# The second block's attention probabilities: transposed by VectorE and a trip through DRAM in place of TensorE

## The chip, the cores and the metric

The kernel runs on one core of a Trainium2 chip. The metric is the time of the program on the device, in microseconds (us); the median over a few runs is compared. TensorE multiplies matrices and writes to PSUM; VectorE, ScalarE and GpSimd (POOL in the rows) work element by element; SyncE (SP) issues the DMA transfers here, in the order of its queue.

## The reference

Three stages follow each other. Attention over 4 sequences of 576 positions, 8 heads of 64, where a position sees itself and the 63 before it:

```python
scores = scale * np.matmul(q, k.transpose(0, 1, 3, 2))
mask = (rel >= 0) & (rel < 64)
scores = np.where(mask, scores, -1e9)
attn = softmax(scores)                  # over the last axis
attn_out = np.matmul(attn, v)
```

Its output, 2304 tokens of 512 numbers, goes through `softplus(x @ w_in) @ w_out` with 2048 inner numbers, and then through `(sigmoid(x @ w_gate) * (x @ w_val)) @ w_out2` with 1536. The weights come in as 64-bit floats, all else as 32-bit floats.

## The kernel before

**The work and its tiles.** The 2304 tokens of the first two stages are cut into blocks of 512, 384, 384, 512 and 512 tokens (L21). For each block and each of 16 slices of the inner dimension there are two slots of TensorE work: a projection (`m1_proj`, L415) and, two slices later, the output product (`m1_out`, L438), each 12 matmuls. Matmuls are done as three products of values split in a high and a low part (`mm3`, L393). The list `slots` (L589 to L614) holds this order; slots 0 to 29 are block 0's but for its last two products, and slot 30 is block 1's first projection. The third stage follows, with a scheme of seven products in place of eight.

**The weights.** Two slices of weights at a time are loaded by SP (`w_load`), and turned from 64-bit floats to 32-bit floats by ScalarE (`w_scale`) and VectorE (`w_shift`, `w_sign`, `w_low`, L159 to L174); then ScalarE casts the high part (`w_hi`, L179) and VectorE subtracts it to give the low part (`w_lo`, L187). For the first stage's 32 slices all of this happens while block 0 runs.

**The attention** goes by groups of 64 queries, all heads at once; block 1 has six groups, 8 to 13, in three pairs. While one block's slots run, the next block's attention is done between them. A group is a chain: scores on TensorE (`att_scores`, L281), scale, mask and maximum on VectorE (`att_max`, L303 and L306), exponentials on ScalarE (`att_exp`, L316), sums and reciprocals on VectorE (`att_sum`, L324 and L325), normalization on GpSimd (`att_norm`, L330). Then the probabilities have to be transposed, in one of two ways:

- *near*, for blocks 0 and 1: four transposes on TensorE into PSUM (`att_transpose`, L338) and a copy from PSUM to SBUF by ScalarE or VectorE (`att_copy`, L367);
- *far*, for block 2 and on (`FAR = 2`, L26): VectorE transposes blocks of 32x32 (`att_blocks`, L346), SP sends the result to DRAM (`att_send`, L352), and SP fetches it in another order by up to four transfers (`att_fetch`, L359), so that the whole is transposed.

After this come the product with the values (`att_values`, L376) and the split of its output into the next block's input (`att_hi`, L384, and `att_lo`, L389). Block 0's own attention is done ahead of the slots, in another set of PSUM banks. Group 9 begins a sequence and has 64 keys in place of 128, so it has half the work in most steps. Scores, near transposes and value products of block 1 and on share two PSUM banks (`at`). The far way's 32x32 result has one buffer (`pd`), normalized probabilities have two.

**The order.** Everything but the slots is first put at a slot by hand. `attention(g, t, far)` (L649) hangs a group's steps on slot `t` and those after it: for the near way the transposes at t + 6 and the values at t + 8, for the far way the block transpose at t + 5 (t + 7 for the pair's second group), the send one slot later, the fetch three after that, and the values at t + 13. The loop at L670 chooses `t` for each pair of a block. Then, for all that lies ahead of the third stage, `lead_in` (L944) plans the order on each engine anew. It takes each step's price, engine, dependencies and buffers from `traits` (L786), goes through the engines' time step by step, and takes among the steps that can start soonest the one with the smallest rank. The rank of a step of weights is worked back from the slot that needs them; the rank of a step of block 1's attention is the time of the slot at which it was put. The engines then run in the order so found, each waiting at its head. What `traits` says of a group's scores and of the buffer of its probabilities depends on `turned(g)` (L781): the step that empties the probabilities, the TensorE transpose or the block transpose.

Of the kernel before, what the change touches and what calls it, by code (L numbers as in the profile page):

```python
# [22 lines left out]
LAG = 2  # L23
LEAD = 7
COMBO0, COMBO = 36, 9.8
FAR = 2  # L26
RG = 1.1
HURRY = 1.0
SLACK, NEAR = 0.15, .3
# [12 lines left out]
def tile_kernel(ctx: ExitStack, tc: tile.TileContext, qk, vt, w1, w2, wg, wv, wo, out):  # L42
# [576 lines left out]
    def at(slot, order, fn, *args):  # L619
        events[slot].append((order, len(events[slot]), fn, args))  # L620
# [28 lines left out]
    def attention(g, t, far):  # L649
        at(t, 20, att_scores, g)  # L650
        at(t + 1, -30, att_max, g)
        at(t + 2, -30, att_exp, g)
        near, odd = g < NG0, g % 2
        at(t + 4 - near, -33, att_sum, g)
        at(t + 4 - near, -32, att_norm, g)
        if far:
            at(t + 5 + 2 * odd, -31, att_blocks, g)
            at(t + 6 + 2 * odd, -61, att_send, g)
            at(t + 9 + 2 * odd, -61, att_fetch, g)
            e = t + 13  # L660
        else:
            e = t + 6 if near else t + 8
            at(e - 2, 21, att_transpose, g)
            at(e - 1, -31, att_copy, g)
        at(e - 4, -59, v_load, g)
        at(e, 22, att_values, g)
        at(e + 1, -29, att_hi, g)
        at(e + 1, -28, att_lo, g)

    for b in range(1, NB1):  # L670
        s0, s1 = pos[m1_proj, b - 1, 0], pos[m1_proj, b, 0]
        ng, g0 = BLOCKS1[b] // Q, starts1[b] // Q
        for j in range(ng):
            far = b >= FAR
            first = -3 if far else 9
            t = s0 + first + (s1 - s0 - (14 if far else 15 + first)) * (j // 2) // max(ng // 2 - 1, 1)
            attention(g0 + j, t, far)
            at(t - 4, -60, qk_load, g0 + j)

# [17 lines left out]
    def used_last(slot):  # L697
        return max(pos[m1_proj if kind == "w1" else m1_out, NB1 - 1, f]
                   for (kind, f), _ in seq1[slot - slot % 2:slot - slot % 2 + 2])

    for f in range(NF2):
        t, i = COMBO0 + int(COMBO * f), len(seq1) + 2 * f
# [12 lines left out]
    for f in range(NF2):  # L715
        i = WO_AT + f
        t = end + (-7, -1)[f] if f < 2 else pos[m2_out, 0, f - 2, 0] - 1
# [11 lines left out]
    for s in range(NS2):  # L729
        t = last + 2 if s == 0 else pos[m2_prod, s - 1, 3, 0]  # L730
# [5 lines left out]
    for k in range(7):  # L736
        for kc in range(2):
            t = max(used_last(2 * k + kc) + 1, last + 18 + k)
# [26 lines left out]
    first = -int(RG * NG0) - 6  # L765
    for g in range(NG0):
        t = int(first + RG * g)
# [13 lines left out]
    def turned(g):  # L781
        return (att_blocks if grp_block[g][0] >= FAR else att_transpose, g)

# [293 lines left out]
```

## Time and profile before

| | |
|---|---|
| runs | 894.48, 894.54, 895.28 us; median 894.54 |
| profiled execution | span from the first to the last instruction 892.8 us; the page gives no other time for it |
| TensorE clock | granted at full speed (2.4 GHz) throughout |
| instructions | 13509 |
| TensorE matmuls | 884.1 us busy, 99% of the span |
| VectorE | 523.7 us, 59% |
| ScalarE | 399.6 us, 45% |
| GpSimd | 153.7 us, 17% |
| the chain that ended last | TensorE 98%, ScalarE 1%, VectorE 1% |
| DMA | 177.59 MB, mean 199 GB/s |

The page is one profiled execution. Busy shares are means over the span, whose stretches differ, and TensorE's busy time is modelled from pipelined matmuls: the start of one to the start of the next is what one costs. What a change in one stretch is worth is read from the rows of that stretch, and from which wait ends last there. In a row of the timeline the start and the duration stand ahead of the engine; a bracket gives the idle time of the engine before it, and who ended it.

### The profile page before, as it was taken

The numbers are of one execution on the slowest core, as the hardware profiler recorded it, in microseconds if no ns is written. First come the engines' busy times: TensorE is split into PE (matmuls) and PEld (weight loads), VectorE is DVE, ScalarE is ACT, GpSimd is POOL, SyncE is SP. The second block draws the span as 40 slices with busy tenths as digits, with TensorE's granted clock in tenths as the row PEclk, the third lists the DMA queues.
The fourth block names the chain that finished last, engine by engine and source line by source line (L and its number), as shares of the span: only waits on it lengthen the run. The fifth ranks groups of instructions, "written<-read, shape, count | busy, mean of one in ns | idle before, by whom it ended". The sixth has DMA issues, their size and how long they took to land.

```text
span 892.8 us, 13509 instructions
## 1 busy us (share of the span) xinstructions
PE 884.1 (99%) x5033; PEld 796.5 (89%) x5035; DVE 523.7 (59%) x921; ACT 399.6 (45%) x892; POOL 153.7 (17%) x157
## 2 busy tenths in 40 slices
PE   9999999999999999999999999999999999999998
PEld 7688789999999888888889999999999999999997
DVE  5898876556555656365515667668445447444444
ACT  6867857546764755345323333334222225222222
POOL 4001102102110220002001333331111112111110
PEclk9999999999999999999999999999999999999999
DMA  9946346766786775683306565545454445544441
GB/s 348 395 158 207 134 163 211 248 198 229 265 270 208 239 235 163 212 284 130 130 1 255 221 256 201 206 176 216 178 212 156 161 163 208 185 165 165 165 166 72
DMA packets 56211, 177.59 MB, mean 199 GB/s; under 512 B 6096, under 2 KB 21456, under 8 KB 51536
## 3 DMA queue, kind: packets, MB, share of 16 engines
q1 hardware_dynamic: 56000, 176.58, 55.9%
q8 instruction: 40, 0.66, 0.3%
q14 instruction: 27, 0.22, 0.1%
q10 hardware_dynamic: 144, 0.13, 0.0%
HBM read 139.72 MB, written 36.96 MB: 198 GB/s over the span
## 4 chain that ended last, share of the span: by engine, by line
PE 98%; ACT 1%; DVE 1%; POOL 0%; issue 0%; POOLq 0%
PE h L394 17%; PE h L396 17%; PE h L395 17%; PE acc L394 11%; PE acc L395 11%; PE acc L396 11%; PE at L289 3%; PE at L376 2%; PE at L396 2%; PE at L395 2%; PE at L394 2%; PE acc L289 1%; PE h L406 1%; PE acc L338 0%; ACT w L179 0%; POOL w L330 0%
## 5 line engine op out<-in xcount | busy, mean ns | idle before, releaser
L512 DVE TENSOR_TENSOR w<-h,w 128x384 f32<-128x384 f32 x216 | 117.1, 556 | 159.5 <-PE h L396 156.8
L394 PE MATMUL h<-w,wc 128*128 128x384 f32 x504 | 169.0, 335 | 0.1
L396 PE MATMUL h<-w,wc 128*128 128x384 f32 x504 | 168.9, 335 | 0.0
L395 PE MATMUL h<-w,wc 128*128 128x384 f32 x504 | 168.7, 335 | 0.0
L524 POOL TENSOR_TENSOR g<-w,g 128x384 fp32r<-128x384 f32 x70 | 73.9, 1056 | 296.7 <-ACT g L517 252.1
L394 PE MATMUL h<-xt,w 128*128 128x512 f32 (+1 forms) x320 | 119.4, 373 | 0.6 <-ACT w L179 0.5
L394 PE MATMUL acc<-g,w 128*128 128x512 f32 (+1 forms) x320 | 119.5, 374 | 0.0
L396 PE MATMUL h<-xt,w 128*128 128x512 f32 (+1 forms) x320 | 117.9, 368 | 1.0 <-DVE w L187 1.0
L396 PE MATMUL acc<-g,w 128*128 128x512 f32 (+1 forms) x320 | 117.7, 368 | 0.0
L395 PE MATMUL acc<-g,w 128*128 128x512 f32 (+1 forms) x320 | 117.6, 368 | 0.0
L395 PE MATMUL h<-xt,w 128*128 128x512 f32 (+1 forms) x320 | 117.6, 368 | 0.0
L436 DVE TENSOR_TENSOR g<-h,g 128x512 fp32r<-128x512 f32 (+1 forms) x80 | 50.7, 634 | 82.9 <-ACT g L430 82.6
L394 PEld LDWEIGHTS h<-w,wc 128*128 128x128 f32 x504 | 94.6, 188 | 2.3 <-DVE w L512 0.4
L395 PEld LDWEIGHTS h<-w,wc 128*128 128x128 f32 x504 | 94.6, 188 | 2.0
L396 PEld LDWEIGHTS h<-w,wc 128*128 128x128 f32 x504 | 94.6, 188 | 0.0
L423 ACT ACTIVATE h<-h 128x512 f32<-128x512 f32 (+1 forms) x80 | 43.2, 540 | 106.6 <-PE h L396 104.4
L517 ACT CAST g<-w 128x384 fp32r<-128x384 f32 x72 | 36.9, 513 | 118.5 <-DVE w L512 118.5
L396 PEld LDWEIGHTS h<-xt,w 128*128 128x128 f32 x320 | 60.0, 188 | 9.5 <-DVE w L187 2.0
L394 PEld LDWEIGHTS h<-xt,w 128*128 128x128 f32 x320 | 60.1, 188 | 9.0 <-ACT w L179 0.6
L394 PEld LDWEIGHTS acc<-g,w 128*128 128x128 f32 x320 | 60.1, 188 | 8.0
L396 PEld LDWEIGHTS acc<-g,w 128*128 128x128 f32 x320 | 60.1, 188 | 7.7
L330 POOL TENSOR_TENSOR p<-p,st 128x512 f32<-128x512 f32 (+1 forms) x28 | 27.8, 996 | 226.8 <-DVE st L325 151.4
(129 smaller groups left out, 1438.5 us busy)
## 6 DMA issues: line engine op xcount, KB each, us to landing
wc<-wcd SPq DMA_DIRECT2D x36, 1792.0 KB, 7.2
qk<-in_qk SPq DMA_DIRECT2D x28, 512.0 KB, 4.8
wcd<-raw SPq DMA_DIRECT2D x24, 512.0 KB, 3.3
w<-in_w SPq DMA_DIRECT2D x16, 512.0 KB, 9.4
raw<-in_w SPq DMA_DIRECT2D x16, 512.0 KB, 4.6
v<-in_vt SPq DMA_DIRECT2D x25, 256.0 KB, 3.7
raw<-in_wg SPq DMA_DIRECT2D x12, 512.0 KB, 4.7
raw<-in_wv SPq DMA_DIRECT2D x12, 512.0 KB, 6.1
```

Of the source, the lines that this page charges most:

```text
L289: nc.tensor.matmul(out=s[:, j, :w], lhsT=t[:, 0, j, :], rhs=t[:, 1, j, :w], start=g >= NG0, stop=g >= NG0 or j == NPAIR - 1)
L330: nc.gpsimd.tensor_tensor(out=p[:, :, :w], in0=p[:, :, :w], in1=st[:, 2, :].unsqueeze(2).to_broadcast([P, NPAIR, w]), op=ALU.mult)
L376: nc.tensor.matmul(out=o[h * Q:(h + 1) * Q, j, :], lhsT=v[:w, (2 * j + h) * Q:(2 * j + h + 1) * Q], rhs=pt[:w, h, j], start=True, stop=True)
L394: nc.tensor.matmul(out=o, lhsT=lh, rhs=rh, start=first, stop=False)
L395: nc.tensor.matmul(out=o, lhsT=lh, rhs=rl, start=False, stop=False)
L396: nc.tensor.matmul(out=o, lhsT=ll, rhs=rh, start=False, stop=last)
L406: nc.tensor.matmul(out=idle["out"], lhsT=t[:, 0, :P], rhs=t[:, 1], start=True, stop=True)
L423: nc.scalar.activation(out=t, in_=t, func=AF.Softplus)
L436: nc.vector.tensor_tensor(out=g[:, 1, :n], in0=t, in1=g[:, 0, :n].bitcast(F32), op=ALU.subtract)
L512: nc.vector.tensor_tensor(out=out, in0=a, in1=b, op=op)
L517: nc.scalar.copy(out=g[:, 0, :HALF], in_=t)
L524: eng.tensor_tensor(out=g[:, 1, :HALF], in0=t, in1=g[:, 0, :HALF].bitcast(F32), op=ALU.subtract)
```

## The change

`FAR` becomes 1, so that block 1's six groups take the far way too, and `turned` and the planner's prices with it. The loop that chooses the slots gets numbers of its own for block 1: the three pairs start at slots 3, 6 and 10, where they started at 9, 12 and 15; their values are put at slots 16, 19 and 23, where they were at 17, 20 and 23. Blocks 2 to 4 keep their slots. The loads of queries and keys are put four slots ahead of the scores, as before.

```diff
--- before.py
+++ after.py
@@ -23,7 +23,7 @@
 LAG = 2
 LEAD = 7
 COMBO0, COMBO = 36, 9.8
-FAR = 2
+FAR = 1
 RG = 1.1
 HURRY = 1.0
 SLACK, NEAR = 0.15, .3
@@ -672,8 +672,8 @@
         ng, g0 = BLOCKS1[b] // Q, starts1[b] // Q
         for j in range(ng):
             far = b >= FAR
-            first = -3 if far else 9
-            t = s0 + first + (s1 - s0 - (14 if far else 15 + first)) * (j // 2) // max(ng // 2 - 1, 1)
+            first = -3 if b > 1 else 3
+            t = s0 + first + (s1 - s0 - (14 if b > 1 else 20 + first)) * (j // 2) // max(ng // 2 - 1, 1)
             attention(g0 + j, t, far)
             at(t - 4, -60, qk_load, g0 + j)
 
```

## Rows read from the trace of the kernel before

**Rows 1.** The page: busy time, share of the span and instructions.

```profile
PE 884.1 (99%) x5033; PEld 796.5 (89%) x5035; DVE 523.7 (59%) x921; ACT 399.6 (45%) x892; POOL 153.7 (17%) x157
```

**Rows 2.** Stretches: length, busy time (instructions) by engine, PEclk, DMA share, GB/s.

```profile
46.60:88.60 42.00, 42.00 (x219) 34.73 (x219) 39.90 (x61) 29.70 (x63) 1.97 (x3) 1.00 0.52 182
...
94.00:129.00 35.00, 34.77 (x222) 28.57 (x223) 28.75 (x44) 23.08 (x44) 2.04 (x2) 1.00 0.52 181
```

**Rows 3.** Timeline of TensorE, and one row of VectorE: start, duration, instruction.

```profile
35.64 1.89 PE L289 MATMUL at<-qk 128*128 128x128 f32 x16
...
96.66 1.95 PE L289 MATMUL at<-qk 128*128 128x128 f32 x16
98.36 0.48 PE L394 MATMUL acc<-g,w 128*128 128x512 f32 x1
...
116.78 0.42 DVE L389 TENSOR_TENSOR xt<-at,xt 128x256 fp32r<-128x256 f32 x1
...
129.07 0.33 PE L394 MATMUL h<-xt,w 128*128 128x384 f32 x1
```

**Rows 4.** Waits from 30 to 130 us (last row: whole span): total, times, longest.

```profile
ACT w L160 <- DMA w<-in_w: 1.7, 2, 0.9
...
PE h L396 <- DVE w L187: 1.0, 1, 1.0
...
PE h L394 <- ACT w L179: 0.5, 1, 0.5
...
SPq L135 <- DVE w L173: 41.1, 8, 12.6
...
DVE pd L346 <- DMA pd<-pd: 4.9, 2, 4.3
```

**Rows 5.** Timeline of TensorE around the wait and an earlier projection.

```profile
85.35 0.50 PE L394 MATMUL h<-xt,w 128*128 128x512 f32 x1
...
94.23 0.50 PE L396 MATMUL h<-xt,w 128*128 128x512 f32 x1 [0.96 <-DVE w L187]
```

**Rows 6.** Timeline of VectorE, 69 to 96 us.

```profile
69.94 0.69 DVE L436 TENSOR_TENSOR g<-h,g 128x512 fp32r<-128x512 f32 x1 [1.37 <-ACT g L430]
...
81.52 0.68 DVE L303 SCALAR_TENSOR_TENSOR p<-at,mask 128x512 f32<-128x512 f32 x1
82.24 0.69 DVE L306 TENSOR_REDUCE st<-p 128x4 f32<-128x512 f32 x1
...
84.76 0.68 DVE L187 TENSOR_TENSOR w<-w,w 128x512 fp32r<-128x512 f32 x1
...
89.43 0.43 DVE L389 TENSOR_TENSOR xt<-at,xt 128x256 fp32r<-128x256 f32 x1 [0.78 <-ACT xt L384]
...
93.50 2.60 DVE L187 TENSOR_TENSOR w<-w,w 128x512 fp32r<-128x512 f32 x4
```

**Rows 7.** Block 1's transposes (median ns in the middle), and one group's neighbours in time.

```profile
L338 PE MATMUL at<-ident,p x24: 270/272/273, 76.5 to 111.8; 128*128 128x128 f32 x20, 128*64 128x128 f32 x4
...
108.07 0.39 PE L396 MATMUL acc<-g,w 128*128 128x512 f32 x1
108.30 0.60 PE L338 MATMUL at<-ident,p 128*128 128x128 f32 x4
108.66 0.48 PE L394 MATMUL h<-xt,w 128*128 128x512 f32 x1
108.97 0.40 PE L395 MATMUL h<-xt,w 128*128 128x512 f32 x1
```

**Rows 8.** The copies of the transposed probabilities.

```profile
L367 ACT COPY pt<-at x6: 580/590/604, 77.1 to 112.1; 128x512 f32<-128x512 f32 x5, 64x512 f32<-64x512 f32 x1
```

**Rows 9.** The later blocks' block transposes, sends and fetches: ns minimum/median/maximum.

```profile
L359 SPq DMA_DIRECT2D pt<-pd x84: 303/427/1682, 136.3 to 365.7; - x84
L346 DVE STREAM_TRANSPOSE pd<-p x22: 445/699/711, 133.5 to 357.0; 128x512 f32<-128x512 f32 x20, 128x256 f32<-128x256 f32 x2
...
DMA to landing us min/median/max: 1.7/3.0/6.9
```

## The prediction

> **What bounds the kernel now.** I read the page first. TensorE is busy for 99% of the span [rows 1], so a saving counts only where TensorE would otherwise go straight on, and a delay counts only where it makes TensorE wait. Next I cut the span with the view of stretches [rows 2]. Block 0's slots end at 129.07 us, where block 1's first projection starts [rows 3]; the change lies before that. In the middle stretch, 46.6 to 88.6 us, TensorE is busy for all 42.00 us, but VectorE is busy for 39.90 us too: it turns weights, splits activations and does the attention's reductions. From 94 to 129 us VectorE has 28.75 of 35 us. So two engines are close to binding up to about 94 us, and only TensorE after that. Last come the waits: between 30 and 130 us TensorE waits twice, 0.5 us for a cast by ScalarE and 1.0 us for a VectorE split of weights [rows 4], the latter at 94.23 us [rows 5].
>
> That second wait shows the mechanism. On VectorE, the low parts of the weights (L187) are ready just when TensorE wants them: one starts at 84.76 us for the projection that starts at 85.35 us, and four start at 93.50 us for the projection whose third matmul goes at 94.23 us [rows 5, 6]. After 46.6 us the two longest idle stretches of VectorE up to there are 1.37 us at 69.94 and 0.78 us at 89.43 [rows 6].
>
> **The sum is made against the profiled execution.** Its span is 892.8 us; the median of the runs is 894.54, so 1.74 us lie around the span, and I carry them over unchanged.
>
> **What is removed.** TensorE loses 24 transposes, four for each of block 1's six groups [rows 7]. The price of four alone: they start at 108.30 us and the next projection at 108.66, which is 0.36 us; the matmul behind comes 0.31 us later where neighbours come after 0.23, another 0.08 [rows 7]. That is 0.44 us a group, 6 x 0.44 = 2.64 us in all; by pairs, 1.76 us of it lie before 94 us and 0.88 us after. ScalarE loses six copies out of PSUM, 590 ns each [rows 8], 3.5 us. No TensorE wait here hangs on them, so I price them at nothing; their bound is the time by which they might hold up another cast on ScalarE, and the wait at 94.23 us (1.0 us) is the most that could give.
>
> **What is added on VectorE.** Six block transposes, five of 699 ns and one (group 9, half as wide) of 445 ns [rows 9]: 3.9 us. Those of the first two pairs, 3 x 0.70 + 0.45 = 2.55 us, are due before 94 us, in the stretch where VectorE has almost no room; those of the third pair, 1.4 us, can fall in the roomy one. Bounds: at nothing, if they all fall into VectorE's waits; at the whole 3.9 us, if every one pushes weights. Nearest to the stretch in question are the two idle rows: 1.37 + 0.78 = 2.15 us of waits into which a 0.7 us instruction fits. I take it that they fill. Then VectorE reaches the wait at 94 us 2.55 - 2.15 = 0.4 us later than before, and since VectorE ends last there, the 1.76 us that TensorE saves ahead of it are worth nothing. After it TensorE binds, and the third pair's 0.88 us are gained in full.
>
> **What is added on the queues.** Six sends and, counting two for group 9, 22 fetches: 28 issues by SP at the fetches' median of 0.43, 12 us [rows 9]. SP issues in order; behind a send that waits for VectorE stand loads of weights. But those loads themselves stood waiting for VectorE for 41.1 us in this stretch [rows 4], so I price the issues at nothing; without that cover a late load costs about what late loads already did, 1.7 us in two waits of ScalarE for weights [rows 4]. Bytes are no question: the DMA engines are 52% busy from 46.6 to 129 us [rows 2].
>
> **What waits longer.** The turned block has one buffer, so the odd group's block transpose waits until the even group's send has landed. In the later blocks that cost VectorE 4.9 us in two waits, the longest 4.3 [rows 4], over 22 block transposes [rows 9]; here weights would stand behind it. The added path from block transpose to values is 0.70 + 0.43 + 3.0 to land + four issues 1.7 + 3.0 = 8.8 us [rows 9]. It has the room: the last of block 1's inputs are split at 116.78 us and used from 129.07 us, 12.3 us later [rows 3], and the slots put the first two pairs' values one slot earlier and the third's where they were.
>
> **What is moved.** Scores and softmax of the three pairs go from slots 9, 12 and 15 to 3, 6 and 10, with their queries and keys; all of this is the same instructions. The first pair's scores already run at 35.64 us, ahead of the 0.5 us wait for weights [rows 3, 4], and its move costs nothing: the cover is that wait. The later pairs' are the risk. Each pair costs VectorE twice the two instructions from 81.52 us, which start 0.72 us apart [rows 6], some 2.7 us, and TensorE 1.70 us for scores (96.66 to 98.36 us [rows 3]). If the third pair's 2.7 us move ahead of weights due at 94 us, they load the full stretch and free the roomy one. Bounds of the move: nothing, or 2.7 - 1.7 = 1.0 us (TensorE has its 1.70 us earlier as well). I take nothing, since the second pair's softmax was itself late, at 81.52 us [rows 6], and weights may go first.
>
> Sum: +0.4 - 0.88 = -0.5 us, 894.54 - 0.5 = **894.1 us**; alone this forecast ranges from 892.8 to 896.3. What a measurement of this kernel can tell from no change is about 0.2%, 1.8 us.
>
> **Rivals.**
> **VectorE has room after all.** Its order is planned anew, and block transposes go into short waits; fewer uses of the two shared PSUM banks help. Then TensorE gains the whole 2.64 us, perhaps with the 1.0 us wait: 891.9 us, at best 890.9. For it: only 1.5 us of TensorE waits in 100 us [rows 4], and ScalarE is relieved. Against: 39.90 of 42 us [rows 2]. Chance 0.33.
>
> **VectorE becomes the bound of block 0: slower.** The place is the weights due at about 94 us. If no idle time is filled and the third pair's softmax comes ahead of them, VectorE is late by 2.55 + 2.7 = 5.25 us there, and TensorE has 0.88 + 1.70 = 2.6 us less to do after that: +2.7, **897.2 us**. It decides from the point where more than 4.4 us (2.6 + 1.8) of VectorE's work are put ahead of those weights without filling a wait. Against: the planner may put weights first. Chance 0.21.
> The Trainium skill's page VectorE: DVE Perf Modes (Rules for kernel authors) says that a 128x128 transpose belongs on TensorE where a PSUM destination will do; by that rule the change trades a cheaper operation for a dearer one and falls on this side. The rows agree on the size, 0.44 us on TensorE against 0.70 us on VectorE [rows 7, 9], though not that both engines' time is worth the same.
>
> **A send holds VectorE.** One pair's second block transpose waits for the first's send as long as it once did, 4.3 us, with weights behind it; -2.64 + 4.3 gives 896.2 us, with a second such wait (4.9 in all) 896.8. Chance 0.06.
>
> **How the numbers follow.** Forecast 0.40, all of it within 0.2%; rivals 0.33, 0.21 and 0.06. Faster by over 0.2%: 0.33; within: 0.40; slower: 0.27. The range takes the forecast whole, the better part of the first rival and the second past its price by 0.4 us: 891.6 to 897.6 us.
>
> **What would show it.** In the profile after: no transposes at L338 on the shared banks after 30 us; 28 block transposes in place of 22, the first at about 55 us; VectorE nearly without idle rows from 46 to 94 us; block 1's first projection within 1 us of 129.07. Wrong, if that projection starts 2 us or more earlier (VectorE had room) or later, with TensorE waits on L187 growing past 3 us (VectorE binds) or a wait of L346 for its send before 129 us (the third rival). If the difference arises behind 129 us, none of these was it.

## The result, and the profile after

The changed kernel takes 901.79 us (median of 4 runs, 901.22 to 902.48) against 894.75 us for the kernel before in the same comparison (894.48 to 895.28): a ratio of 1.0077, with a 95% interval of 1.0066 to 1.0089. It is 7.0 us slower; 894.1 us was predicted, with a range of 891.6 to 897.6. The profiled execution is the one of 901.22 us, with a span of 899.2 us, 6.4 more than before.

The page of the kernel after, its row of busy time, answers to [rows 1]:

```profile
PE 884.7 (98%) x5009; PEld 794.4 (88%) x5011; DVE 530.1 (59%) x929; ACT 396.0 (44%) x886; POOL 151.1 (17%) x155
```

The 24 transposes are gone (5033 - 5009); VectorE has eight instructions more, the six block transposes and two splits of the third stage's weights that the planner took from GpSimd. Yet TensorE is busy 0.6 us longer, and the span has grown by 6.4 us. TensorE's timeline in the kernel after shows where (rows 3 and 5 have the same for before):

```profile
30.16 0.47 PE L394 MATMUL h<-xt,w 128*128 128x512 f32 x1 [0.15 <-PE h L406]
...
51.29 0.50 PE L394 MATMUL h<-xt,w 128*128 128x512 f32 x1 [1.64 <-ACT w L179]
...
76.68 0.50 PE L396 MATMUL acc<-g,w 128*128 128x512 f32 x1 [2.34 <-DVE w L187]
...
78.17 0.62 PE L396 MATMUL acc<-g,w 128*128 128x512 f32 x1
78.59 0.63 PE L394 MATMUL acc<-g,w 128*128 128x512 f32 x1
79.02 0.63 PE L395 MATMUL acc<-g,w 128*128 128x512 f32 x1
...
106.09 0.50 PE L396 MATMUL h<-xt,w 128*128 128x512 f32 x1 [1.97 <-DVE w L187]
...
135.20 0.33 PE L394 MATMUL h<-xt,w 128*128 128x384 f32 x1
```

Block 1's first projection starts at 135.20 us, where it was 129.07 [rows 3]: 6.1 of the 6.4 us arise in block 0. Three waits for weights carry it, at 51, 77 and 106 us; before there was one of 0.96 us at 94 [rows 5]. The waits of the same stretch, 30 to 136 us (total, times, longest), as in [rows 4]:

```profile
DVE st L324 <- ACT p L316: 2.7, 3, 1.2
...
PE acc L396 <- DVE w L187: 2.3, 1, 2.3
...
ACT bits L160 <- DMA w<-in_w: 2.2, 2, 1.4
...
PE h L394 <- ACT w L179: 2.2, 3, 1.6
PE h L396 <- DVE w L187: 2.1, 2, 2.0
...
ACT w L160 <- DMA w<-in_w: 0.9, 1, 0.9
...
DVE pd L346 <- POOL p L330: 0.7, 1, 0.7
```

No block transpose waits for a send here. Late loads cost ScalarE 2.2 + 0.9 = 3.1 us; before, it was 1.7 us [rows 4] and 1.3 more for loads into other tiles, 3.0 in all. In this kernel neither the one buffer nor the queue of transfers is the cause. The stretches of the kernel after (length, busy time by engine, PEclk, DMA share, GB/s), the first as in [rows 2]:

```profile
46.60:88.60 42.00, 37.59 (x176) 29.00 (x174) 36.15 (x55) 27.79 (x60) 3.69 (x4) 0.96 0.58 191
...
78.00:81.60 3.60, 3.60 (x15) 3.17 (x14) 2.28 (x4) 1.22 (x3) 0.00 (x0) 0.53 0.75 256
```

Two things stand here that the prediction did not have. VectorE is **less** busy than before in the stretch that it was to bound, 36.15 of 42 us against 39.90: it waits itself while TensorE waits for it. And from 78.0 to 81.6 us the granted clock is 0.53, which is the lower level (1.2 GHz); the matmuls at 78.17, 78.59 and 79.02 us start 0.42 to 0.43 us apart, where those before them start 0.23 apart.

Block 0's slots, from the first projection of block 0 to that of block 1, divide as follows. Idle is the length less TensorE's busy time in that stretch; the loss to the clock is the sum, over windows of 0.5 us, of the window times one less its PEclk.

| kernel | length of block 0, us | TensorE idle | lost to the clock | VectorE busy |
|---|---|---|---|---|
| before | 98.98 | 1.45 | 0 | 87.13 |
| after | 105.04 | 7.21 | 1.71 | 91.16 |

Of the +6.06 us, waits are +5.76 and the clock +1.71, less 2.64 for the transposes; the other 1.2 were not followed up (the first matmul behind each wait takes 0.34 us to the next, where others take 0.23; more of it may lie in scores issued one group at a time).

**What TensorE waits for.** VectorE's timeline in the kernel after, ahead of the waits at 77 and at 106 us:

```profile
69.97 0.69 DVE L187 TENSOR_TENSOR w<-w,w 128x512 fp32r<-128x512 f32 x1
70.58 0.69 DVE L164 TENSOR_SCALAR w<-w 128x1024 uint32<-128x1024 uint32 x1
...
72.94 0.17 DVE L324 TENSOR_SCALAR st<-st 128x4 f32<-128x4 f32 x1 [0.41 <-ACT p L316]
...
74.49 0.17 DVE L324 TENSOR_SCALAR st<-st 128x4 f32<-128x4 f32 x1 [1.16 <-ACT p L316]
...
74.79 0.70 DVE L346 STREAM_TRANSPOSE pd<-p 128x512 f32<-128x512 f32 x1
75.41 1.22 DVE L187 TENSOR_TENSOR w<-w,w 128x512 fp32r<-128x512 f32 x1
...
102.02 0.42 DVE L389 TENSOR_TENSOR xt<-at,xt 128x256 fp32r<-128x256 f32 x1 [0.77 <-ACT xt L384]
102.36 1.22 DVE L168 SCALAR_TENSOR_TENSOR w<-w,w 128x1024 uint32<-128x1024 uint32 x1
103.61 1.23 DVE L173 SCALAR_TENSOR_TENSOR w<-w,w 128x1024 uint32<-128x1024 uint32 x1
104.75 0.68 DVE L436 TENSOR_TENSOR g<-h,g 128x512 fp32r<-128x512 f32 x1
105.35 0.68 DVE L187 TENSOR_TENSOR w<-w,w 128x512 fp32r<-128x512 f32 x1
```

and ScalarE's and GpSimd's in the same kernel:

```profile
45.55 1.28 ACT L316 ACT_TABLE_LOAD   x1
...
50.21 1.03 ACT L179 CAST w<-bits 128x1024 fp32r<-128x1024 f32 x1
...
68.90 1.05 ACT L179 CAST w<-w 128x1024 fp32r<-128x1024 f32 x1
...
75.04 1.04 POOL L330 TENSOR_TENSOR p<-p,st 128x512 f32<-128x512 f32 x1 [0.51 <-DVE st L325]
...
100.12 1.03 ACT L179 CAST w<-w 128x1024 fp32r<-128x1024 f32 x1
```

The L187 at 75.41 us, for which TensorE waits until 76.68, splits a high part whose cast ended at 69.95. It stands in VectorE's queue behind two sums (L324) that wait 0.41 and 1.16 us for exponentials, and behind a block transpose; and then it takes 1.22 us where the same instruction at 69.97 takes 0.69, while GpSimd normalizes (75.04 to 76.08 us). The one at 105.35 us had its cast at 101.15 and stands behind a wait of 0.77 us and 3.1 us of other weights' and activations' work. At 51 us it is ScalarE: the first pair's exponentials, moved forward, run with a table load from 45.55 us up to the cast at 50.21 for which TensorE waits until 51.29; the input of that cast was there from 48.18 us, when VectorE's L173 ended. So at 77 us, and in part at 106, ready weights stand behind work that is not ready, and at 51 us behind work that runs but could wait: it is the order that makes them late at these three places.

### The profile page after: what moved, and what is told of

Read it like the earlier page. It is cut to its first block, busy times and chain, and to the rows that moved or that the text cites. A ratio compares the mean times of both kernels' runs of the same rounds, so it can differ in the third digit from the quotient of the medians.

```text
span 899.2 us, 13478 instructions
## 1 busy us (share of the span) xinstructions
PE 884.7 (98%) x5009; PEld 794.4 (88%) x5011; DVE 530.1 (59%) x929; ACT 396.0 (44%) x886; POOL 151.1 (17%) x155
## 4 chain that ended last, share of the span: by engine, by line
PE 91%; DMA 5%; ACT 2%; DVE 1%; issue 1%; SPq 0%; ACTq 0%
PE h L394 17%; PE h L396 17%; PE h L395 16%; PE acc L394 11%; PE acc L396 11%; PE acc L395 11%; DMA w<-in_w 3%; PE at L289 2%; PE at L396 2%; PE at L395 2%; PE at L394 2%; PE at L376 2%; DMA w<-in_vt 1%; DMA w<-in_qk 1%; ACT p L316 0%
## 5 line engine op out<-in xcount | busy, mean ns | idle before, releaser
L436 DVE TENSOR_TENSOR g<-h,g 128x512 fp32r<-128x512 f32 (+1 forms) x80 | 50.6, 634 | 83.3 <-ACT g L430 83.1
```

Source lines behind the costliest of these rows:

```text
L436: nc.vector.tensor_tensor(out=g[:, 1, :n], in0=t, in1=g[:, 0, :n].bitcast(F32), op=ALU.subtract)
```

## The experiments

The theories, as the expectations name them: **C**, capacity: the 3.9 us that VectorE gets are what the change costs. **Q**: the earlier slots of the scores and softmax make the loss. **H**, head of the queue: VectorE waits for exponentials with ready weights behind it. When these three had each explained a part at most, a fourth came: the order that the planner finds is itself the cost, and **any** change of the plan's inputs would cost about as much (**P**, the plan, in the expectations; **F** is its opposite, that the far way itself costs the 7 us). Diffs are against the kernel after or before, as said. Ratios are to the kernel before, run beside each; its median was 894.69 to 895.16 us. Where the waits or the length of a block are given, they are of one profiled execution of each kernel.

**far_old**: the kernel after with the near way's slots.

```diff
-            first = -3 if b > 1 else 3
-            t = s0 + first + (s1 - s0 - (14 if b > 1 else 20 + first)) * ...
+            first = -3 if b > 1 else 9
+            t = s0 + first + (s1 - s0 - (14 if b > 1 else 15 + first)) * ...
```

> Block 1 goes the far way, at the slots of before (9, 12, 15). Theory Q (queues: the early slots put exponentials, sums and block transposes ahead of weights in the in-order queues of ScalarE and VectorE, where they wait for each other): the waits at 51, 77 and 106 us go, time 892 to 895 us, at or below before. Theory C (capacity: the 3.9 us of block transposes on VectorE are what makes weights late): still slow, 898 to 902 us.

904.47 us, 1.0105 [1.0089, 1.0121]: slower still, and above what either theory said. Q alone is wrong, since the slots are back and the loss stays. TensorE waits 2.23 us at 90.32 and 2.77 us at 98.49, in other places than in the kernel after, in the same way. VectorE's timeline of far_old ahead of these two:

```profile
87.41 0.28 DVE L324 TENSOR_SCALAR st<-st 128x4 f32<-128x4 f32 x1 [0.96 <-ACT p L316]
...
87.82 0.70 DVE L346 STREAM_TRANSPOSE pd<-p 128x512 f32<-128x512 f32 x1
88.44 1.22 DVE L164 TENSOR_SCALAR w<-w 128x1024 uint32<-128x1024 uint32 x1
89.59 0.68 DVE L187 TENSOR_TENSOR w<-w,w 128x512 fp32r<-128x512 f32 x1
...
95.29 0.69 DVE L303 SCALAR_TENSOR_TENSOR p<-at,mask 128x512 f32<-128x512 f32 x1 [1.54 <-PE at L289]
```

The second is a softmax step that waits 1.54 us for TensorE's scores, with weights behind it for which TensorE then waits: each engine is held by the other.

**near_new**: the kernel before (TensorE transposes) with the new slots.

```diff
-            first = -3 if far else 9
-            t = s0 + first + (s1 - s0 - (14 if far else 15 + first)) * ...
+            first = -3 if b > 1 else 3
+            t = s0 + first + (s1 - s0 - (14 if b > 1 else 20 + first)) * ...
```

> Block 1 keeps TensorE's transposes, at the early slots (3, 6, 10). Theory Q: as slow as the changed kernel or slower by the transposes' 2.6 us, 899 to 904 us. Theory C: as before, 894 to 896 us.

902.08 us, 1.0079 [1.0064, 1.0094]: as slow as the change, with not one block transpose added. So C alone is wrong too. But the loss lies elsewhere. In the profiled execution (900.27 us, the fastest of the four) block 0 takes 100.91 us (+1.93, of which +1.76 idle), it starts 1.1 us later, and a later block waits 1.25 us for an activation's cast. Two rows of TensorE's timeline in near_new:

```profile
52.19 0.50 PE L394 MATMUL h<-xt,w 128*128 128x512 f32 x1 [2.54 <-ACT w L179]
...
290.54 0.51 PE L394 MATMUL h<-xt,w 128*128 128x512 f32 x1 [1.25 <-ACT xt L384]
```

**dup**: the kernel after, with block 1's block transposes done twice.

```diff
-        nc.vector.transpose(out=d[...], in_=p[...])
+        for _ in range(2 if grp_block[g][0] == 1 else 1):
+            nc.vector.transpose(out=d[...], in_=p[...])
```

> The changed kernel with each of block 1's six block transposes issued twice, same plan of the order. Theory C: another 3 to 4 us, 905 us. Theory Q: VectorE sits idle in its queue anyway, so part of it falls into waits: under 2 us more, 902 to 903.5 us.

902.91 us, 1.0090 [1.0075, 1.0105], 1.1 us more than the kernel after, a difference that the two intervals do not separate. In the traces block 0 grows by 1.58 us (106.62) for 3.4 us more of VectorE's work (94.54 us busy): by this one pair of executions VectorE's time has a price of somewhat under half, not the whole that C alone wants.

**before_extra**: the kernel before, whose near transposes are each joined by a block transpose into a tile that nobody reads; the planner does not know of it, so the order stays that of before.

```diff
+        if grp_block[g][0] == 1:
+            d = late["apool"].tile([P, 4, NPAIR, 32], F32, tag="pd", ...)
+            nc.vector.transpose(out=d[:, :w // 32]..., in_=p[:, :, :w]...)
```

> The kernel before, with one block transpose more on VectorE for each of block 1's groups, that nobody reads (3.9 us in all), same plan of the order. Theory C: 3 to 4 us slower, 898 us. Theory Q: at most 1.5 us slower, under 896.3 us.

897.42 us, 1.0029 [1.0019, 1.0038]: +2.6 us, of which 1.88 in block 0 (100.86), between what C and Q said. This is the added VectorE work alone, at before's order and without TensorE's saving. One row of TensorE's timeline, and VectorE's busy time in the stretch of [rows 2], both of before_extra (its line numbers are 4 higher):

```profile
96.17 0.50 PE L400 MATMUL h<-xt,w 128*128 128x512 f32 x1 [1.98 <-DVE w L187]
```

```profile
46.60:88.60 42.00, 41.67 (x209) 34.37 (x208) 39.91 (x58) 29.62 (x62) 1.61 (x2) 1.00 0.52 182
```

The wait of 0.96 us at 94 us [rows 5] becomes 1.98 us at 96, with a new one of 0.33 at 86.72: the very place the second rival named, at less than its price. VectorE's busy time in the stretch does not grow (39.91 of 42 us, 39.90 before), though two of the added block transposes run there (77.09 and 78.82 us): other work comes later for them.

**nowait** and **nowait_old**: the kernel after, and far_old, where block 1's sums read the maxima and the block transpose reads a constant, so that neither waits for ScalarE or GpSimd. Block 1's probabilities are thereby not what is multiplied.

```diff
-            nc.vector.tensor_scalar(out=st[:, 1, :], in0=st[:, 1, :], ...)
-        nc.vector.reciprocal(out=st[:, 2, :], in_=st[:, 1, :])
+            k = 0 if grp_block[g][0] == 1 else 1
+            nc.vector.tensor_scalar(out=st[:, 2, :], in0=st[:, k, :], ...)
+        nc.vector.reciprocal(out=st[:, 2, :], in_=st[:, 1 if g < NG0 else 2, :])
...
-                            in_=p[:, :, :width(g)]...
+                            in_=(p[:, :, :width(g)] if grp_block[g][0] != 1 else ident[...]...)...
```

> The changed kernel, its plan of the order untouched, but in block 1 the sums on VectorE read the maxima and the block transposes read a constant, so neither waits for the exponentials and the normalization any more; block 1's probabilities are not what is multiplied. Theory H (head of line: sums and block transposes that wait stand ahead of weights that are ready): the waits at 77 and 106 us shrink and TensorE's low clock after the first goes, 895 to 898 us; the wait at 51 us stays. Theory C (capacity: VectorE simply has too much to do, now as before): 900 us or more.

> The same two cuts in the kernel with the far way at the slots of before. Theory H: the waits at 90 and 98 us shrink to those of capacity, 895 to 899 us. Theory C: 902 us or more.

nowait: 900.29 us, 1.0057 [1.0040, 1.0073], 1.5 us better than the kernel after, which the intervals do not quite separate. nowait_old: 905.04 us, 1.0109 [1.0094, 1.0125], no better than far_old. TensorE's waits from 30 to 136 us in nowait (its line numbers are 1 higher):

```profile
PE h L395 <- ACT w L179: 2.6, 2, 1.7
PE h L397 <- DVE w L187: 2.1, 2, 2.0
PE acc L397 <- DVE w L187: 1.0, 2, 0.6
```

The wait at 77 us has shrunk to two short ones (2.3 to 1.0 us in all), the other two are where they were. The low clock has not gone but moved: it now falls behind the wait of 1.97 us at 104.28, and costs block 0 the same 1.71 us.

```profile
105.70:109.10 3.40, 3.40 (x10) 0.50 0.47 144
```

(nowait, TensorE alone: length, busy time, PEclk, DMA share, GB/s.) H is a true reading of that one wait and not the cause of the loss. Both times lie where C had put them, 900 and 902 us or more.

**putoff**: the kernel after, with block 1's sums, normalizations and block transposes ranked 6 us later in the plan, so that weights pass them.

```diff
-                    nodes[fn, *args] = [us + order / 400, *traits(fn, *args)]
+                    put_off = 6.0 * (fn in (att_sum, att_norm, att_blocks) and grp_block[args[0]][0] == 1)
+                    nodes[fn, *args] = [us + order / 400 + put_off, *traits(fn, *args)]
```

> The changed kernel with the planner's rank of block 1's sums, normalizations and block transposes put off by 6 us, so that weights go first. Theory H: fewer waits behind them, 896 to 899 us. Theory C: the same work in the same stretch, 900 us or more.

904.60 us, 1.0105 [1.0082, 1.0127]. Not a cure, and again on C's side: one wait for L187 is now 4.0 us long.

**mid**: the kernel after, the pairs at slots 6, 9 and 12 (`first` 6, `18 + first`).

> The far way with the three pairs at slots 6, 9 and 12, between the two choices. If the wait at 51 us is the early first pair's alone, it goes; the waits behind block transposes stay: 898 to 902 us. If a good choice of slots is all that is lacking, 892 to 895 us.

900.82 us, 1.0062 [1.0044, 1.0080]. Between the two sets of slots in place, and not distinguishable from the better of them. The wait at 51 us is gone, so that one was the early first pair's. In the profiled execution (903.05 us, the slowest of the four) TensorE waits 1.19 us at 82.24 us for a fetch of block 1's own probabilities, which it does nowhere in the kernel after:

```profile
82.24 0.68 PE L376 MATMUL at<-pt,v 64*64 64x64 f32 x16 [1.19 <-DMA pt<-pd]
```

By then every edit that made the planner plan anew had cost 5 to 10 us, whichever way turned the probabilities. That led to the control that should have come first.

**before_hurry**: the kernel before, one constant of the planner changed (`HURRY` ranks the weights of later slices earlier). Nothing is added or removed. But the planner also chooses the engine of some steps, and so not quite "the same to the last instruction": one copy of block 1's transposed probabilities goes from ScalarE to VectorE, and two splits of the third stage's weights from GpSimd to VectorE.

```diff
-HURRY = 1.0
+HURRY = 1.1
```

> The kernel before, with one constant of the planner changed (HURRY 1.0 to 1.1, which moves the due times of the later weights by up to 0.1 us): the work is the same to the last instruction, its order is planned anew. Theory P (the plan: the order of before is a well chosen one, and any other order costs several us): 3 to 9 us slower, 898 to 904 us, with TensorE waits for weights in block 0 and perhaps behind. Theory F (the far way itself costs the 7 us): within 1 us of before.

902.22 us, 1.0081 [1.0066, 1.0096]: a loss as large as the change's, from the order and these three instructions. But it falls in block 1, which takes 83.94 us where it took 77.36; block 0 takes only 0.81 us longer. A row of TensorE's timeline and two stretches of before_hurry:

```profile
134.09 0.50 PE L394 MATMUL acc<-g,w 128*128 128x512 f32 x1 [1.91 <-ACT w L179]
```

```profile
134.00:138.00 4.00, 3.41 (x9) 2.44 (x10) 3.02 (x5) 3.31 (x5) 0.72 (x1) 0.73 0.27 95
138.00:142.00 4.00, 4.00 (x22) 3.67 (x21) 3.05 (x4) 0.38 (x1) 0.00 (x0) 0.84 0.34 106
```

Again weights behind an attention's exponentials, and again the clock falls after the wait. The value was taken because its order differs much from before's; it is one bad order, and does not say how many are bad.

**far_best1, far_best2, near_best**: other orders for the far way and for the near way. Several constants of the planner at once, the slots, and for far_best1 one slot instead of two between the block transposes of a pair; the sets were chosen by the planner's own forecast of the time.

```diff
far_best1 (after): HURRY 0.7; SLACK, NEAR 0.1, 0.2; MARGIN 1.2; FLIP 5.0; LATE 1.0; pairs at slots 6, 8, 10
far_best2 (after): HURRY 0.7; SLACK, NEAR 0.1, 0.3; MARGIN 1.2; FLIP 6.0; LATE 1.5; pairs at slots 2, 6, 11
near_best (before): HURRY 0.7; SLACK, NEAR 0.15, 0.3; MARGIN 1.2; FLIP 7.0; LATE 1.0; pairs at slots 9, 10, 11
```

> The far way for block 1 with five constants of the planner and the slots (6, 8, 10) chosen anew. Theory P: most of the loss comes back, 893 to 897 us; what is left over that of before is VectorE's added time. Theory F: 899 us or more.

> The far way with another such choice (slots 2, 6, 11). Theory P: 893 to 898 us. Theory F: 899 us or more.

> TensorE's transposes for block 1, with four constants of the planner and the slots (9, 10, 11) chosen anew. Theory P: as before or up to 2 us faster, 892 to 896 us. Theory F says nothing of it.

far_best1: 899.60 us, 1.0048 [1.0032, 1.0065]. far_best2: 897.07 us, 1.0030 [1.0014, 1.0046]. near_best: 896.25 us, 1.0016 [1.0007, 1.0026]. By the expectations far_best2 sides with P, far_best1 with F, and near_best lies just above what P said: the planner's forecast is no sure guide. far_best2 transposes every block as the kernel after does, and loses 2.2 us where the kernel after loses 7.0. Its block 0 runs from 30.92 to 129.61 us, 98.69 us and so 0.29 shorter than before's; TensorE waits 4.41 us there and is 3.25 less busy. The 2.2 us lie around it: block 0 starts 0.83 us later, and the two blocks behind it take 0.72 and 1.18 us longer. The stretch of [rows 2] in far_best2:

```profile
46.60:88.60 42.00, 39.57 (x225) 31.64 (x224) 40.64 (x60) 29.72 (x59) 4.03 (x4) 1.00 0.68 229
```

VectorE is busy 40.64 of 42 us here, with the clock at 1.00: of the 2.1 us that it had free in this stretch, 0.7 are filled. In all of block 0 VectorE is busy for 91.87 us, more than in the kernel after (91.16), in a block that is 6.35 us shorter. So the 105 us of the kernel after are not what VectorE's work needs, which C alone would have.

**third** and **third_ctl**: the far way for the third pair alone, groups 12 and 13, where VectorE has room [rows 2]; and its control, with the same constants and the near way throughout.

```diff
both, against before:
-HURRY = 1.0
+HURRY = 1.3
-FLYING, SWITCH, MARGIN, FLIP, LATE = 10, 1.3, 1.5, 6.0, 2.0
+FLYING, SWITCH, MARGIN, FLIP, LATE = 10, 1.3, 1.5, 6.0, 1.0
third alone:
+            if b == 1 and g0 + j in (12, 13):
+                far, t = True, 14
...
-        return (att_blocks if grp_block[g][0] >= FAR else att_transpose, g)
+        return (att_blocks if grp_block[g][0] >= FAR or g in (12, 13) else att_transpose, g)
```

> The kernel before with two constants of the planner changed (HURRY 1.3, LATE 1.0), the control for the next run. Theory P: another order, 0 to 4 us slower than before, by the waits that it happens to bring.

> The control, with the far way for block 1's third pair alone (groups 12 and 13, put at slot 14), behind the stretch that VectorE fills. If VectorE has room there, as I predicted, the pair's 0.88 us of TensorE transposes are gained against the control: 0.5 to 1.5 us faster than it, perhaps faster than before. If block transposes hurt there too, it is 1 us or more slower than the control.

third_ctl: 897.43 us, 1.0030 [1.0018, 1.0042]. third: 894.11 us, 0.9993 [0.9984, 1.0001], which is the same as before, and shown neither faster nor slower. The first rows of block 0 and of block 1 on TensorE's timeline, third and then third_ctl:

```profile
31.28 0.47 PE L394 MATMUL h<-xt,w 128*128 128x512 f32 x1
...
128.68 0.33 PE L394 MATMUL h<-xt,w 128*128 128x384 f32 x1
```

```profile
31.26 0.47 PE L394 MATMUL h<-xt,w 128*128 128x512 f32 x1
...
129.63 0.33 PE L394 MATMUL h<-xt,w 128*128 128x384 f32 x1
```

Block 0 takes 97.40 us against 98.37: 0.97 us gained for eight transposes moved. TensorE is idle in both for 1.2 us and busy for 0.93 us less, so the gain is its own work saved. The rest of the 3.3 us between the two lies behind block 0, 1.4 of it a wait of the control in block 2 (at 248.37 us, for VectorE's L436) that third does not have, and so not the transposes' gain.

## Why the prediction was wrong

**The step that failed is "What is moved".** It priced the move of the scores and softmax at nothing, 1.0 us at most, as "the same instructions", and the whole sum took before's order as given, with the added and removed work laid into it. But the order is planned anew from all prices and slots, and what an order is worth stood in no term. The runs size it: the same work of the far way, but for two or three steps that the planner gave to another engine, takes 897.07 to 904.60 us in six orders, and far_best2, with other slots and constants, loses 2.2 us where the change loses 7.0. About 5 of the change's 7 us thus hang on its order. The new slots alone, with TensorE's transposes, cost 7.3 us (near_new), not 1.0 at most.

That is not to say that any new order would cost as much, with or without the change. The time over before's, for the whole (medians) and for block 0 (profiled executions):

| kernel | whole, us | block 0, us | VectorE busy in block 0, us |
|---|---|---|---|
| near way: near_new | +7.3 | +1.93 | 87.24 |
| before_hurry | +7.4 | +0.81 | 87.06 |
| near_best | +1.4 | +1.49 | 89.15 |
| third_ctl | +2.7 | -0.61 | 88.25 |
| far way: after | +7.0 | +6.06 | 91.16 |
| far_old | +9.7 | +4.72 | 91.02 |
| putoff | +9.4 | +4.87 | 91.54 |
| mid | +5.7 | +4.92 | 90.60 |
| far_best1 | +4.8 | +5.23 | 92.34 |
| far_best2 | +2.2 | -0.29 | 91.87 |

near_new and before_hurry match the change's total, but lose it mostly outside block 0, where the change loses almost nothing; that their totals agree with its 7.0 us is in part chance. In block 0 no order of the near way loses over 1.93 us, and five of six of the far way lose 4.7 or more. So a bad order and a fuller VectorE seem to go together there. far_best2 shows that the far way need not lose; why the other five orders do, and whether the fuller VectorE makes good orders rare, is open.

**What is removed, 2.64 us,** was right. Where VectorE had room the third pair's share was forecast at 0.88 us, and third against third_ctl gives 0.97 in block 0.

**What is added on VectorE** was sized low. Bounds were 0 and 3.9 us, and 2.15 us were taken to fill idle time ahead of 94 us, leaving 0.4 there. before_extra measures the added work at 1.88 us in block 0 and 2.6 in all; its first block transpose comes at 77.09 us, and of the two idle rows the 1.37 us stands as 1.36 and the 0.78 us as 0.47. Against TensorE's 2.64 us, 1.88 to 2.6 us leave -0.8 to 0; by the prediction's own argument, that TensorE's 1.76 us ahead of 94 us are worth nothing, +1.0 and more. far_best2's block 0 is at -0.29. So the forecast of -0.5 us is not far from what the change may do apart from its order, but not by the sum that gave it. That before_extra's time and the 2.64 would add up in one and the same order was not shown: no kernel has the far way in before's order.

**What is added on the queues** and **what waits longer** were right at nothing in this kernel: late loads cost 3.1 us where they cost 3.0, and no block transpose waits for a send before 129 us. The third rival did not occur. In another order of the far way the added path can cost, as mid's 1.19 us for a fetch show.

**VectorE becomes the bound** (0.21) had the sign, and by the mark set for it, waits on L187 over 3 us (2.3 + 2.1), it is the rival that came nearest. Its mechanism, though, was another: 5.25 us of work at one place, 94 us, on a VectorE without idle time. The wait at 94 is gone; VectorE is busy 3.75 us less in that stretch, where it was to have hardly an idle row; the waits lie at 51, 77 and 106 us, and the first is ScalarE's. It said 897.2 us. That before_extra comes to 897.42 does not bear it out: that kernel has neither the moved softmax nor TensorE's saving, which both stand in the rival's sum.
The rule cited beside it was that a full 128x128 transpose belongs on TensorE where PSUM will do (the Trainium skill, VectorE: DVE Perf Modes, Rules for kernel authors). The runs do not decide on it for all six groups: VectorE's added time costs block 0 1.88 us (before_extra), TensorE's transposes 2.64 us by the rows, and no two kernels set the one against the other in the same order. Where VectorE has room they go against it (third, 0.97 us gained in block 0).

**The clock** stood in no term. It cost some 1.71 us in the kernel after, by its PEclk. No run separates it; the figure is worked out from the rows.

**What stays open.** The orders run are few: five of the near way (ratios 1 to 1.0081) and six of the far way (1.0030 to 1.0105), nowait and third apart. That the far way's best would stay 2 us behind the near way's best is not shown. A second buffer for the turned block was not tried. No version was clearly faster than the kernel before.

## What to carry to other kernels

Where an order is planned, and two engines are nearly full, a change's time is that of the order it gets: price the edit, but run a control that only disturbs the plan, before any theory of the edit itself, and compare where the two lose, not only how much. Read whether the late engine is busy or waiting: ready work behind work that is not ready is the order's doing. Move work only where the receiving engine has room in that stretch, pair by pair rather than all at once.

## What the runs showed of the hardware

**TensorE's clock fell with some waits and not with others.** In the kernel after, behind 2.34 us without a matmul, those from 76.68 us start 0.23 us apart for 1.5 us and then 0.42 apart until about 81.4, at PEclk 0.53, the lower level. In before_hurry (1.91 us at 134 us; PEclk 0.73 and 0.84 over the next 8 us) and nowait (1.97 us at 104.28) the fall too comes after matmuls have resumed, and so it does in mid behind 1.19 us at 82.24 (PEclk 0.51 from 83.6 to 90.5 us). In far_old the clock is down as they resume, behind 2.23 us:

```profile
90.32 0.79 PE L396 MATMUL acc<-g,w 128*128 128x512 f32 x1 [2.23 <-DVE w L187]
90.91 0.63 PE L394 MATMUL acc<-g,w 128*128 128x512 f32 x1
```

The waits of 1.64 and 1.97 us at 51 and 106 us in the kernel after brought none, nor did 2.77 us at 98.49 in far_old and 2.54 us at 52.19 in near_new (TensorE alone: length, busy time, PEclk, DMA share, GB/s):

```profile
52.20:56.20 4.00, 3.82 (x16) 1.00 0.07 15
```

So in these traces the length of a wait does not by itself say whether the clock falls.

**VectorE's L187 and L164 took longer beside GpSimd's normalization.** L187 took 1.22 us at 75.41 beside GpSimd's 75.04 to 76.08, where the 20 of this form in the kernel before, none of them beside a normalization, took 0.68 to 0.69 us; in far_old L164, 0.69 us at 70.58 in the kernel after, took 1.22 at 88.44 beside GpSimd's 88.08 to 89.12. In the kernel after this lengthened the wait at 77 us by an estimated 0.5 us (1.22 - 0.69). The Trainium skill (SBUF — State Buffer, Terms) says that the two engines share a pair of ports, which one instruction at a time holds; these rows agree.
